# Attention and a feed-forward layer in one kernel: one head's softmax scaling in late turns goes from the vector engine to GpSimd, and head 1 is turned first

## The chip, the core and the metric

The kernel runs on one core of a Trainium2 chip. The core has five engines that each work through a queue of their own in order: TensorE (PE, matrix products; its weight loads are listed as PEld), the vector engine (DVE), ScalarE (ACT), GpSimd (POOL) and SyncE (SP, which here only issues DMAs). They meet through semaphores. The metric is the device time of one execution in microseconds; for the kernel before it is the median of three runs.

## The reference

Two stages, everything in fp32. Shapes: q, k and v are (8 batches, 8 heads, 576 positions, 64); w_in is (512, 2048), w_out is (2048, 512).

```python
scores = (q @ k.T) / 8                      # per batch and head, 576 x 576
mask   = (pos[:, None] // 64) >= (pos[None, :] // 64)
scores = where(mask, scores, -1e9)
attn   = exp(scores - max(scores))
attn   = attn / (sum(attn) + 1e-9)
x      = (attn @ v), heads side by side     # (4608, 512)
h      = x @ w_in
out    = (h * sigmoid(1.702 * h)) @ w_out   # (4608, 512)
```

The mask is causal by blocks of 64, so of a row of queries only the keys up to the end of its own block count.

## The kernel before

**Attention.** Heads go in pairs, and a pair is a turn: 32 turns, numbered n. The 576 queries of a head are cut in five chunks, 0 to 4; chunk i has 128 queries (chunk 0 has 64) and needs 64 x (2i + 1) keys, so chunk 4 needs all 576. For each chunk `score` puts the scores of both heads into PSUM, `weigh` applies mask and scale and takes the row's extreme on the vector engine (L351) and the exponential with its row sum on ScalarE (L358), and `normalise` adds 1e-9 to the sum, doubles it (which halves h, so that (1 + tanh(1.702 h/2)) h/2 is h x sigmoid) and takes the reciprocal on the vector engine (L368, L371) and multiplies each head's weights by it (L376 on GpSimd, L378 on the vector engine, L380 on ScalarE). The table `SCALE_ON` says which engine does that for each chunk, in three phases: turns 0 to 3, 4 to 7, and the 24 late turns from 8 on. Before the change GpSimd has all of it but chunk 4 of the late turns, where the vector engine scales both heads.

**Turning the weights.** The product with v needs the weights with the keys on the partitions. In the first eight turns TensorE transposes them. In the late turns `turn` does it: the vector engine transposes blocks of 32x32 into the tile `turned`, one instruction for each head (L385) and one for the diagonal blocks of both heads (L390), and after chunk 4 sixteen DMAs on SyncE's queue (L397) move the blocks to their places in the other half of `turned`. The next turn's `av` (60 matmuls) reads them there. Chunk 0 has no L385.

**Feed-forward.** It runs between the pieces of attention, in 12 tiles of 384 tokens and 16 chunks of 128 columns for each. For one such chunk TensorE makes 12 products into `hp`, ScalarE a tanh (L562), the vector engine `g = (g + 1) * hp` (L563); ScalarE splits off a high part `gh` (L571), GpSimd the low part `gl` (L82, through `subtract`), and TensorE adds 9 products of the chunk before into `acc`. There is one PSUM bank for `hp`, so the products of the next chunk wait until L563 has read the last.

**What sets the order.** A turn's items stand in strings, for late turns

```python
"3+0/2+1 - - - V - - 4 - - - L -"
```

that is: chunks 3 and 0 in one bank and 2 and 1 in the next, `av` of the turn before (V), chunk 4, and loading and turning the next pair's q and k (L, `prep`, whose vector work is L297). Feed-forward work fills the slots after a time plan (`quota`, `advance`). Matrix products are held to the order of the program (`mm`, `tr`). All other instructions are ordered on their engines by the framework's planner, which simulates the program and issues what is ready, by priority; priority is the place in the program, and L562, L563, L571 and `gl` are raised by `high_priority(offset=300)`.

Of the kernel before, what the change touches and what calls it, by code (L numbers as in the profile page):

```python
# [16 lines left out]

SCALE_ON = ("PPPPP", "PPPPP", "PPPPD")  # L20

# [17 lines left out]
def attention_moe_kernel(  # L41
# [10 lines left out]
    B, H, S, D = q.shape  # L52
    DM, DF = w_in.shape
    P = 128
# [23 lines left out]
    def phase(n):  # L78
        return 0 if n < HP else 1 if n < 2 * HP else 2
# [85 lines left out]
    def width(i):  # L165
        return BLK * (2 * i + 1)
# [138 lines left out]
    def score(n, banks):  # L305
# [25 lines left out]
        for chunks, part in zip(banks, todo):  # L331
            e = {}
            for i, hd, lo, hi, s in part:
                e[i] = weigh(n, i, hd, lo, hi, s, e.get(i))
            for i in chunks[::-1]:
                normalise(n, i, e[i])
                if not early(n):
                    turn(n, i, e[i])
# [25 lines left out]
    def normalise(n, i, e):  # L364
        _, sm = stats[n]
        m = BLK if i == 0 else P
        c = sm[0:m, i]
        nc.vector.tensor_scalar(  # L368
            out=c, in0=c, scalar1=1e-9, scalar2=2.0, op0=ALU.add, op1=ALU.mult
        )  # L370
        nc.vector.reciprocal(out=c, in_=c)  # L371
        on = SCALE_ON[phase(n)][i]
        for hd in range(2):
            x, sc = e[0:m, hd], c[:, hd : hd + 1]
            if on == "P":
                nc.gpsimd.tensor_tensor(out=x, in0=x, in1=sc.to_broadcast([m, width(i)]), op=ALU.mult)  # L376
            elif on == "D":
                nc.vector.tensor_scalar(out=x, in0=x, scalar1=sc, scalar2=None, op0=ALU.mult)  # L378
            else:
                nc.scalar.activation(out=x, in_=x, func=AF.Copy, scale=sc)  # L380

    def turn(n, i, e):

        for hd in range(2 if i else 0):
            nc.vector.transpose(  # L385
                out=tw[:, :, SLOT[i] : SLOT[i] + i, hd].rearrange("p b j c -> p j b c"),
                in_=e[:, hd, 0 : i * P],
            )
        r = slice(BLK, P) if i else slice(0, BLK)
        nc.vector.transpose(  # L390
            out=tw[r, 0:2, 9 + max(i, 1)].rearrange("p b h c -> p h b c"), in_=e[r, :, i * P : width(i)]
        )
        if i == NCH - 1:
            for kb in range(4):
                for qb in range(4):
                    ns = 10 if kb > 1 else NS if qb > 1 else 11
                    nc.sync.dma_start(  # L397
                        out=pw[kb * 32 : kb * 32 + 32, qb, 0:ns], in_=tw[qb * 32 : qb * 32 + 32, kb, 0:ns]
                    )
# [265 lines left out]
```

## Time and profile before

| | |
|---|---|
| time, median of 3 runs | 1122.79 us (1121.68 to 1124.22) |
| profiled execution: time, span | 1120.49 us, 1118.6 us |
| busy share of the span: PE, PEld | 96%, 81% |
| DVE, ACT, POOL | 52%, 45%, 36% |
| granted TensorE clock, mean over the span | 0.992 |
| DMA, mean over the span | 82 GB/s |

| stretch, us | what runs | PE busy | DVE busy | ACT busy | POOL busy |
|---|---|---|---|---|---|
| 0 to 195 | turns 0 to 7, weights made | 164.06 | 140.98 | 133.57 | 114.13 |
| 195 to 560 | late turns | 357.99 | 200.25 | 153.94 | 123.19 |
| 592.3 to 960 | late turns | 367.41 | 200.75 | 153.25 | 121.93 |
| 960 to 1118.6 | feed-forward alone | 154.59 | 24.09 | 45.49 | 36.59 |

Busy time is the time in which an engine has an instruction running. Instructions of one engine overlap a little at their ends, and matmuls are pipelined, so a TensorE that is always busy can still have lost some time: the distance between the starts of two neighbouring matmuls shows it better. A bracket at the end of a row of a timeline is idle time of the engine before it and what ended it; where several instructions of one kind follow each other without a gap the row merges them (x2, x3) and gives their time together. Numbers behind a line's name, as 128x576, are partitions by elements.

### The profile page before, as it was taken

The numbers are of one execution on the slowest core, as the hardware profiler recorded it, in microseconds if no ns is written. First come the engines' busy times: TensorE is split into PE (matmuls) and PEld (weight loads), VectorE is DVE, ScalarE is ACT, GpSimd is POOL, SyncE is SP. The second block draws the span as 40 slices with busy tenths as digits, with TensorE's granted clock in tenths as the row PEclk, the third lists the DMA queues.
The fourth block names the chain that finished last, engine by engine and source line by source line (L and its number), as shares of the span: only waits on it lengthen the run. The fifth ranks groups of instructions, "written<-read, shape, count | busy, mean of one in ns | idle before, by whom it ended". The sixth has DMA issues, their size and how long they took to land. (4 is left out here: it accounts for less than half of the span.)

```text
span 1118.6 us, 19977 instructions
## 1 busy us (share of the span) xinstructions
PE 1076.4 (96%) x6960; PEld 908.7 (81%) x6960; DVE 583.0 (52%) x1856; ACT 498.6 (45%) x1321; POOL 406.7 (36%) x509
## 2 busy tenths in 40 slices
PE   5969998999999999999999999999999999999998
PEld 3757776788888888888888888888888888899997
DVE  6776885545545555654555655645545654211210
ACT  5866776434534433534443543444434444322322
POOL 4665664333333332333333333333333233122222
PEclk9979999999999999999999999999999999999999
DMA  8734532332444432343443333344342332200000
GB/s 171 205 89 153 150 73 62 84 79 57 105 86 86 103 80 64 64 98 78 98 101 74 75 93 65 70 108 85 81 107 63 71 85 58 54 29 1 29 1 29
DMA packets 219365, 91.25 MB, mean 82 GB/s; under 512 B 197760, under 2 KB 197760, under 8 KB 219264
## 3 DMA queue, kind: packets, MB, share of 16 engines
q1 hardware_dynamic: 214528, 89.38, 34.0%
q10 hardware_dynamic: 4736, 0.59, 0.3%
q8 instruction: 55, 0.90, 0.3%
q14 instruction: 46, 0.38, 0.1%
HBM read 45.09 MB, written 9.44 MB: 49 GB/s over the span
## 5 line engine op out<-in xcount | busy, mean ns | idle before, releaser
L82 POOL TENSOR_TENSOR gl<-g,gh 128x384 fp32r<-128x384 f32 x192 | 194.7, 1014 | 551.5 <-ACT gh L571 449.1
L99 PE MATMUL hp<-xh,wih 128*128 128x384 f32 x768 | 264.7, 345 | 7.9 <-DVE g L563 6.9
L563 DVE SCALAR_TENSOR_TENSOR g<-g,hp 128x384 f32<-128x384 f32 x192 | 105.9, 552 | 319.1 <-ACT g L562 317.8
L99 PE MATMUL hp<-xh,wil 128*128 128x384 f32 x768 | 258.4, 336 | 0.1
L562 ACT ACTIVATE g<-hp 128x384 f32<-128x384 f32 x192 | 94.1, 490 | 359.8 <-PE hp L99 354.8
L99 PE MATMUL hp<-xl,wih 128*128 128x384 f32 x768 | 253.9, 338 | 0.4 <-DVE xl L82 0.4
L99 PE MATMUL acc<-woh,gh 128*128 128x512 f32 x576 | 233.9, 406 | 0.0
L99 PE MATMUL acc<-wol,gh 128*128 128x512 f32 x576 | 226.9, 394 | 0.0
L99 PEld LDWEIGHTS hp<-xh,wih 128*128 128x128 f32 x768 | 144.2, 188 | 34.1 <-DVE g L563 23.1
L99 PE MATMUL acc<-woh,gl 128*128 128x512 f32 x576 | 167.9, 393 | 0.3 <-POOL gl L82 0.3
L571 ACT CAST gh<-g 128x384 fp32r<-128x384 f32 x192 | 98.4, 513 | 156.5 <-DVE g L563 156.4
L99 PEld LDWEIGHTS hp<-xh,wil 128*128 128x128 f32 x768 | 144.3, 188 | 6.5 <-POOL wil L82 0.7
L358 ACT ACTIVATE e<-e,mx 64x64 f32<-64x64 f32 (+4 forms) x240 | 132.3, 552 | 37.6 <-DVE mx L351 37.6
L376 POOL TENSOR_TENSOR e<-e,sm 64x64 f32<-64x64 f32 (+1 forms) x192 | 113.6, 612 | 95.0 <-DVE sm L371 46.5
L99 PEld LDWEIGHTS hp<-xl,wih 128*128 128x128 f32 x768 | 143.6, 188 | 1.3 <-DVE xl L82 1.3
L99 PE MATMUL bank<-qk 64*128 64x320 f32 (+4 forms) x768 | 122.5, 428 | 14.5 <-DVE qk L297 11.1
L99 PEld LDWEIGHTS acc<-woh,gh 128*128 128x128 f32 x576 | 107.9, 187 | 34.2 <-issue 10.5
L99 PEld LDWEIGHTS acc<-woh,gl 128*128 128x128 f32 x576 | 107.8, 188 | 25.9 <-POOL gl L82 1.2
L99 PEld LDWEIGHTS acc<-wol,gh 128*128 128x128 f32 x576 | 108.3, 188 | 16.7 <-POOL wol L82 0.3
L351 DVE CUSTOM_DVE_ANT_0 e<-bank,mask 64x64 f32<-64x64 f32 (+4 forms) x240 | 89.7, 417 | 56.9 <-PE bank L99 52.8
L385 DVE STREAM_TRANSPOSE turned<-e 128x384 f32<-128x384 f32 (+1 forms) x192 | 92.3, 499 | 48.8 <-POOL e L376 48.3
L99 PEld LDWEIGHTS bank<-qk 64*128 64x128 f32 x768 | 69.6, 193 | 54.2 <-issue 25.4
(50 smaller groups left out, 956.0 us busy)
## 6 DMA issues: line engine op xcount, KB each, us to landing
turned<-turned SPq DMA_DIRECT2D x192, 80.0 KB, 2.1
turned<-turned SPq DMA_DIRECT2D x96, 112.0 KB, 2.2
raw<-in_q_dram SPq DMA_DIRECT2D x128, 72.0 KB, 2.4
out_dram<-osb SPq DMA_DIRECT2D x36, 256.0 KB, 2.2
raw<-in_k_dram SPq DMA_DIRECT2D x120, 72.0 KB, 2.6
turned<-turned SPq DMA_DIRECT2D x96, 88.0 KB, 2.1
words<-in_moe_w_in_dram SPq DMA_DIRECT2D x16, 512.0 KB, 6.3
vp<-in_v_dram SPq DMA_DIRECT2D x60, 128.0 KB, 2.4
```

The lines of the kernel that those rows point to most:

```text
L82: eng.tensor_tensor(out=out, in0=in0, in1=in1, op=ALU.subtract)
L99: return tc.keep_in_program_order(nc.tensor.matmul(**kw))
L351: nc.vector.tensor_tensor_reduce(out=e[0:m, hd, lo:hi], in0=s, in1=mk, op0=ALU.add, op1=ALU.min, scale=-0.125, scalar=3e38 if lo == 0 else ...
L358: nc.scalar.activation(out=e[0:m, hd], in_=e[0:m, hd], func=AF.Exp, scale=-1.0, bias=mx[0:m, i, hd : hd + 1], accum_out=sm[0:m, i, hd : hd ...
L376: nc.gpsimd.tensor_tensor(out=x, in0=x, in1=sc.to_broadcast([m, width(i)]), op=ALU.mult)
L385: nc.vector.transpose(out=tw[:, :, SLOT[i] : SLOT[i] + i, hd].rearrange("p b j c -> p j b c"), in_=e[:, hd, 0 : i * P],)
L562: nc.scalar.activation(out=g, in_=hp[:, 0:tt], func=AF.Tanh, scale=1.702)
L563: nc.vector.scalar_tensor_tensor(out=g, in0=g, scalar=1.0, in1=hp[:, 0:tt], op0=ALU.add, op1=ALU.mult)
L571: nc.scalar.copy(out=gh, in_=g)
```

## The change

In the late turns GpSimd multiplies head 0 of chunk 4 and the vector engine head 1; the letter M in the table stands for that. And `turn` takes head 1 before head 0, for all chunks from 1 to 4 of the late turns.

```diff
-SCALE_ON = ("PPPPP", "PPPPP", "PPPPD")
+SCALE_ON = ("PPPPP", "PPPPP", "PPPPM")
...
         on = SCALE_ON[phase(n)][i]
         for hd in range(2):
             x, sc = e[0:m, hd], c[:, hd : hd + 1]
-            if on == "P":
+            if on == "P" or on == "M" and hd == 0:
                 nc.gpsimd.tensor_tensor(out=x, in0=x, in1=sc.to_broadcast([m, width(i)]), op=ALU.mult)
-            elif on == "D":
+            elif on != "A":
                 nc.vector.tensor_scalar(out=x, in0=x, scalar1=sc, scalar2=None, op0=ALU.mult)
             else:
                 nc.scalar.activation(out=x, in_=x, func=AF.Copy, scale=sc)
 
     def turn(n, i, e):
 
-        for hd in range(2 if i else 0):
+        for hd in (1, 0) if i else ():
             nc.vector.transpose(
```

## Rows read from the trace of the kernel before

**Rows 1.** TensorE's waits, 195 to 960 us: engine, line, releaser, total us, times, longest.
```profile
PE hp L99 <- DVE g L563: 5.1, 6, 0.9
PEld hp L99 <- DVE g L563: 21.0, 40, 1.3
```

**Rows 2.** Vector engine, one turn's chunk 4: start, us, engine, line, tiles, count.
```profile
562.30 1.44 DVE L297 STREAM_TRANSPOSE qk<-raw 128x576 f32<-128x576 f32 x2
...
563.82 0.17 DVE L371 RECIPROCAL sm<-sm 128x2 f32<-128x2 f32 x1
564.02 0.95 DVE L378 TENSOR_SCALAR e<-e,sm 128x576 f32<-128x576 f32 x2
564.88 1.30 DVE L385 STREAM_TRANSPOSE turned<-e 128x512 f32<-128x512 f32 x2
566.21 0.31 DVE L390 STREAM_TRANSPOSE turned<-e 64x128 f32<-64x128 f32 x1
566.55 0.55 DVE L563 SCALAR_TENSOR_TENSOR g<-g,hp 128x384 f32<-128x384 f32 x1
```

**Rows 3.** TensorE in that turn: behind chunk 4, then an undisturbed stretch.
```profile
566.31 0.86 PE L99 MATMUL acc<-woh,gl 128*128 128x512 f32 x3
567.16 0.45 PE L99 MATMUL hp<-xh,wih 128*128 128x384 f32 x1
567.44 0.34 PE L99 MATMUL hp<-xh,wil 128*128 128x384 f32 x1
...
577.15 0.85 PE L99 MATMUL acc<-woh,gl 128*128 128x512 f32 x3
577.85 0.33 PE L99 MATMUL hp<-xh,wih 128*128 128x384 f32 x1
578.02 0.34 PE L99 MATMUL hp<-xh,wil 128*128 128x384 f32 x1
```

**Rows 4.** TensorE behind chunk 4 in an earlier turn.
```profile
277.07 0.86 PE L99 MATMUL acc<-woh,gl 128*128 128x512 f32 x3
278.78 0.45 PE L99 MATMUL hp<-xh,wih 128*128 128x384 f32 x1 [0.85 <-DVE g L563]
```

**Rows 5.** Chunk 2 of a turn: vector engine, and first GpSimd's line.
```profile
586.53 1.40 POOL L376 TENSOR_TENSOR e<-e,sm 128x320 f32<-128x320 f32 x2 [1.22 <-DVE sm L371]
586.22 0.17 DVE L371 RECIPROCAL sm<-sm 128x2 f32<-128x2 f32 x1
...
587.96 0.45 DVE L385 STREAM_TRANSPOSE turned<-e 128x256 f32<-128x256 f32 x1 [0.23 <-POOL e L376]
588.42 0.31 DVE L390 STREAM_TRANSPOSE turned<-e 64x128 f32<-64x128 f32 x1
588.76 0.55 DVE L563 SCALAR_TENSOR_TENSOR g<-g,hp 128x384 f32<-128x384 f32 x1
```

**Rows 6.** GpSimd's groups by shape, 0 to 195 us: busy us, mean ns.
```profile
L376 POOL TENSOR_TENSOR turned<-turned,sm 128x576 f32<-128x576 f32 x16 | 18.0, 1146 | 5.7 <-DVE sm L371 2.6 <-DVE mx L351 2.0 <-ACT xr L450 0.8
```

**Rows 7.** Meetings of the two engines, and the gl's duration min/median/max ns.
```profile
20.69 1.12 DVE L368 TENSOR_SCALAR sm<-sm 64x2 f32<-64x2 f32 x1
20.64 2.25 POOL L376 TENSOR_TENSOR turned<-turned,sm 128x576 f32<-128x576 f32 x2 [1.71 <-DVE sm L371]
212.48 0.95 DVE L378 TENSOR_SCALAR e<-e,sm 128x576 f32<-128x576 f32 x2
213.19 1.12 POOL L82 TENSOR_TENSOR gl<-g,gh 128x384 fp32r<-128x384 f32 x1 [5.54 <-ACT gh L571]
L82 POOL TENSOR_TENSOR gl<-g,gh x141: 991/1013/1117, 198.1 to 958.1; 128x384 fp32r<-128x384 f32 x141
```

**Rows 8.** The vector engine's waits, 195 to 960 us, as in rows 1.
```profile
DVE turned L385 <- POOL e L376: 48.3, 94, 1.1
```

**Rows 9.** SyncE's queue and TensorE behind chunk 4 of the turn in rows 2.
```profile
566.21 11.14 SPq L397 DMA_DIRECT2D turned<-turned  x16
580.04 2.99 PE L99 MATMUL bank<-turned,vp 128*64 128x128 f32 x60
```

## The prediction

> **What bounds the kernel now.** I read the busy shares first, then the windows by stage, then TensorE's waits in the late stretch, and last the instructions of single turns on each engine. TensorE is the bound: in the stretch of the late turns, from 195 to 960 us, there is next to nothing that it waits for except one thing. Before the first matrix product of a feed-forward chunk (hp) it waits for the vector engine's g step (L563), because there is one PSUM bank for hp and that step is the last reader of it; the matmul row has 6 such waits, the weight-load row 40 [rows 1]. So the edit can matter by one road only: what it does to the moment at which L563 gets its turn on the vector engine, which works through its queue in order.
>
> Two queues hold it up. The first is chunk 4's: reciprocal, two scalings, two wide transposes, the transpose of the diagonal, then L563 [rows 2]. The reader is to see that these stand one behind the other with no gap, and that L563 starts 0.03 us after the diagonal's transpose. What it costs TensorE is seen on its own rows [rows 3]. Undisturbed, the first hp product starts 0.70 us after the last three acc products begin (577.15 to 577.85), and the next 0.17 us later. Behind chunk 4 it is 0.85 us (566.31 to 567.16) and 0.28: 0.26 us lost. In other turns the same queue ends later against TensorE and 1.71 us pass (277.07 to 278.78) [rows 4], some 1.0 us lost at the start and 1.1 with the interval behind it. I went through the 24 late turns: the loss is there in 23, about 1.1 in 6 of them, 0.28 in 15, 0.15 in two; 6 x 1.13 + 15 x 0.28 + 2 x 0.15 = 11.3 us. The other queue is that of chunk 2, with L563 right behind its diagonal [rows 5]; in 17 turns it costs 0.15 to 0.4 us, 3.3 in all. 23 and 17 are the 40 waits. In all of these L563 is already late for TensorE, so a shift of L563 passes to the time one for one, later or (until the loss is gone) earlier.
>
> **The change, chunk 4.** Removed from the vector engine: one of two scalings a turn. The pair takes 0.95 us, and the next instruction starts 0.86 after the first of them, so one is worth 0.43 [rows 2]. Added: a GpSimd multiplication of 128x576, 1.146 us in the early turns, where GpSimd has all of chunk 4 [rows 6]; and a wait, of head 0's transpose for it. What stands behind that wait on the vector engine is head 0's transpose, the diagonal (which reads both heads) and L563. Step by step, with the turn at 564 us:
> - The reciprocal ends at 563.82 + 0.17 = 563.99. Head 1's scaling starts at 564.02 as now and, 0.95 - 0.43 = 0.52 long, ends at 564.54. Head 1's transpose starts 0.43 behind the scaling's start, at 564.45, and is over by 565.15.
> - GpSimd starts a scaling 0.14 us after the reciprocal's end (586.22 + 0.17 to 586.53) [rows 5], so head 0's at 564.13, behind the vector engine's scaling, and meets it for 0.41 us.
> - What such a meeting costs is shown once: a GpSimd gl of 1.013 median began at 213.19, 0.24 us before the end of a pair of these scalings (212.48 + 0.95 = 213.43), and took 1.117 [rows 7]. 0.24 of overlap cost 0.10, so the first 0.14 us of the GpSimd instruction need nothing that the vector engine holds. Bounds from these rows: between no slip and the whole overlap, 0.41. I take 0.41 - 0.14 = 0.27, from the one row of this very pair of engines and operations.
> - Head 0's scaling then ends at 564.13 + 1.146 + 0.27 = 565.55. The transpose follows 0.03 later (586.53 + 1.40 to 587.96 [rows 5]), at 565.58. The present pair of transposes takes 1.30, 0.65 each, and they overlap a little; for one alone I take 0.70, an estimate, to 566.28. The diagonal follows 0.01 later (587.96 + 0.45 to 588.42), at 566.29 to 566.30, against 566.21 now: 0.09 us later, and L563 with it.
>
> So the saved 0.43 us is spent by the wait: the vector engine idles some 0.4 us between the two heads' transposes. The sum: 23 turns x 0.09 = 2.1 us slower. With no slip it is 0.27 - 0.09 = 0.18 earlier, with the whole overlap 0.14 more, 0.23 later: -4 to +5 us are the bounds of this term.
>
> The Trainium skill, "SBUF — State Buffer", section "SBUF: two separate sides", has a lock in this place: a port pair of the vector engine and GpSimd, held for the whole instruction by whichever starts first, the other fully blocked. By that rule GpSimd's full 1.146 us would begin at 564.54, which gives 23 x 0.23 = 5.3 us. The row of the GpSimd gl shows less than full blocking, 0.10 for 0.24, so I stay with the row.
>
> What hides the rest: the sixteen DMAs behind the diagonal leave in 11.14 us from 566.21, and their reader, the 60 matmuls of the next turn, starts at 580.04 [rows 9]. 0.09 us later changes nothing there. GpSimd has 1.146 us x 24 = 28 us more to do; its next gl needs the result of L563, which comes later than the end of head 0's scaling.
>
> **The change, chunks 1 to 3.** The turning order is reversed for them too. If the queue took the program's order literally, head 1's transpose would wait for the second GpSimd scaling and head 0's would come after it. But the order on the engine is the planner's, which issues what is ready: in this trace the transposes of the next pair's queries and keys (L297), which the program has behind chunk 4, stand ahead of chunk 4's reciprocal [rows 2]. Nearly all of the transposes of chunks 1 and 2 wait for GpSimd, 94 waits [rows 8], so each is issued as it gets ready, and head 0 is ready first. I take no change here. From both sides: nothing below, since no work goes; above, one transpose's length per chunk, as in the third rival.
>
> **Rivals.**
> 1. GpSimd and the vector engine don't hold each other up here. For: only one row shows the slip. Against: it is this very scaling that caused it. L563 comes 0.18 earlier; 21 x 0.18 + 2 x 0.15 = 4.1 us faster, 1118.7. 12%.
> 2. The planner sees the wait of head 0's transpose and puts L563, which has a raised priority, into it. For: in two turns L563 already stands ahead of the diagonal. Against: in the other 22 it was put behind the whole queue, and the new queue is hardly longer. The most it can give is the 11.3 us of chunk 4's losses: 1111.5; ahead of the diagonal alone, 0.31 - 0.09 = 0.22 a turn, 5 us: 1118. 14%.
> 3. Slower: the new order binds in chunks 1 and 2. Head 1's transpose can't start before 587.96 as now, and head 0's 0.45 follows, so the diagonal and L563 move from 588.42 and 588.76 by 0.45 [rows 5]; chunk 1's, of a transpose shorter than that, is passed on, so up to 0.9. In 17 turns L563 is late there already: 7.7 to 15.3 us, with the 2.1 some 1133 to 1140. It decides as soon as head 0's transpose isn't issued in the gap before head 1's. 14%.
> 4. Slower: GpSimd starts first. A tiny scaling of the vector engine (L368) that began 0.05 us behind a GpSimd pair took 1.12 us: it waited out the whole first instruction (20.64 + 1.146 = 21.79, and it ends at 21.81) [rows 7]. If head 1's scaling met that, it would begin at 564.13 + 1.146 = 565.28 and head 1's transpose at 565.28 + 0.43 = 565.71, where the pair now begins at 564.88: 0.83 late, 23 x 0.83 = 19 us, 1142. Against: head 1's scaling follows the reciprocal on the same engine by 0.03 us, GpSimd by 0.14, and only an instruction put between them would turn that round. By the rule named above the first to start holds the other, too. 6%.
> 5. It does nothing: slip and saving cancel, or the planner's new order gives back what the wait costs. Within 1 us of now. 12%.
>
> **How the numbers follow.** The profiled execution took 1120.49 us (span 1118.6), 2.3 below the median of the runs, 1122.79. The sum of 2.1 on it gives 1122.6; on the median, 1124.9, which I predict (42%). Its own range, 0.04 to 0.15 us a turn, is 1123.7 to 1126.3. The range of 8 in 10 takes in rivals 1, 2 and 5 below and stops short of most of 3 and of 4: 1112 to 1131. About 0.2%, 2.25 us, is what a measurement can tell. Slower by more: rivals 3 and 4 (20%) and 18 of the forecast's 42, which lies just under that bound: 38%. Within: the other 24 and rival 5's 12: 36%. Faster: rivals 1 and 2, 26%.
>
> **What would show it.** In the changed profile: one L378 a turn, with head 1's transpose right behind it; an idle gap of some 0.4 us of the vector engine before head 0's, ended by GpSimd (L376); the 128x576 scaling at 1.40 to 1.45 us instead of 1.146 (no slip: 1.15, the lock's full price: 1.56); 23 losses of TensorE before L563 behind chunk 4, each about 0.09 longer; chunks 1 and 2 as in [rows 5]. I am wrong if L563 stands in another place of the queue, or if that scaling runs at 1.15.

## The result and the profile after

The change makes the kernel slower by about a quarter of a per cent: 1126.10 us (median of 9 runs, 1125.31 to 1128.57) against 1122.94 (9 runs) for the kernel before, a ratio of 1.0028, 95% interval 1.0017 to 1.0040, or 1.9 to 4.5 us. The profiled execution took 1125.38 us, its span is 1123.5.

First the two waits of TensorE that [rows 1] showed and the vector engine's wait of [rows 8] (kernel after, 197 to 965 us: releaser, total us, times, longest).

```profile
PE hp L99 <- DVE g L563: 6.2, 8, 1.0
...
PEld hp L99 <- DVE g L563: 23.6, 40, 1.5
...
DVE turned L385 <- POOL e L376: 55.3, 119, 1.1
```

TensorE's weight loads have 40 waits for L563 as before, and these have become longer in all, 21.0 to 23.6 us; the vector engine has 25 waits more for GpSimd, about one a turn. TensorE has no other new wait of that size. Next the two scalings of chunk 4 (kernel after: by line, duration min/median/max in ns, first and last start; then by group, busy us and mean ns).

```profile
L378 DVE TENSOR_SCALAR e<-e,sm x24: 520/521/1237, 214.9 to 955.7; 128x576 f32<-128x576 f32 x24
```
```profile
L376 POOL TENSOR_TENSOR e<-e,sm 128x576 f32<-128x576 f32 x24 | 33.3, 1386 | 37.6 <-DVE sm L371 37.6
```

One L378 a turn instead of two, and the GpSimd multiplication takes 1386 ns where the same shape undisturbed took 1146 [rows 6]. Now one turn, the one of [rows 2, 3]: the timelines of the vector engine, GpSimd and TensorE (kernel after).

```profile
567.35 0.17 DVE L371 RECIPROCAL sm<-sm 128x2 f32<-128x2 f32 x1
567.55 0.52 DVE L378 TENSOR_SCALAR e<-e,sm 128x576 f32<-128x576 f32 x1
568.10 0.71 DVE L385 STREAM_TRANSPOSE turned<-e 128x512 f32<-128x512 f32 x1
569.10 0.71 DVE L385 STREAM_TRANSPOSE turned<-e 128x512 f32<-128x512 f32 x1 [0.29 <-POOL e L376]
569.84 0.31 DVE L390 STREAM_TRANSPOSE turned<-e 64x128 f32<-64x128 f32 x1
570.18 0.55 DVE L563 SCALAR_TENSOR_TENSOR g<-g,hp 128x384 f32<-128x384 f32 x1
```
```profile
567.68 1.39 POOL L376 TENSOR_TENSOR e<-e,sm 128x576 f32<-128x576 f32 x1 [1.41 <-DVE sm L371]
```
```profile
569.84 0.86 PE L99 MATMUL acc<-woh,gl 128*128 128x512 f32 x3
570.79 0.44 PE L99 MATMUL hp<-xh,wih 128*128 128x384 f32 x1
571.07 0.34 PE L99 MATMUL hp<-xh,wil 128*128 128x384 f32 x1
```

Read them from left to right. The vector engine is done with head 1 at 568.81 and then stands idle 0.29 us until GpSimd hands over head 0. From the start of the reciprocal to the start of L563 it is 567.35 to 570.18, 2.83 us; before it was 563.82 to 566.55, 2.73 [rows 2]. TensorE passes the 0.10 on: from the last acc products to the first of hp 569.84 to 570.79, 0.95, where 0.85 stood [rows 3].

How that adds up is read from one line. L390, the diagonal's transpose, marks the late turns: its first execution opens them, its last one closes the last chunk 4. The kernel before and the kernel after (duration min/median/max in ns, first and last start in us):

```profile
L390 DVE STREAM_TRANSPOSE turned<-e x120: 295/308/311, 194.7 to 952.9; 64x128 f32<-64x128 f32 x120
```
```profile
L390 DVE STREAM_TRANSPOSE turned<-e x120: 297/308/311, 197.2 to 958.0; 64x128 f32<-64x128 f32 x120
```

The late stretch is 952.9 - 194.7 = 758.2 us before and 958.0 - 197.2 = 760.8 after: 2.6 us longer. What follows it is the same (1118.6 - 952.9 = 165.7, 1123.5 - 958.0 = 165.5). What precedes it differs by 2.5 us between these two executions, but it does so between executions of any of the kernels below (194.7 to 199.7, once 199.2 in a kernel with the time of before); the mean granted clock there is 0.96 of full speed in the one and 0.94 in the other. So spans are not compared here, but this stretch is.

Two more places. Chunk 2 of the kernel after, against [rows 5] (vector engine):

```profile
589.82 0.17 DVE L371 RECIPROCAL sm<-sm 128x2 f32<-128x2 f32 x1
590.88 0.45 DVE L385 STREAM_TRANSPOSE turned<-e 128x256 f32<-128x256 f32 x1 [0.90 <-POOL e L376]
591.56 0.45 DVE L385 STREAM_TRANSPOSE turned<-e 128x256 f32<-128x256 f32 x1 [0.23 <-POOL e L376]
...
592.36 0.55 DVE L563 SCALAR_TENSOR_TENSOR g<-g,hp 128x384 f32<-128x384 f32 x1
```

2.54 us from reciprocal to L563, as before (586.22 to 588.76): the reversed order does nothing here. And a turn in which L563 stood ahead of the diagonal, the kernel before and then the kernel after:

```profile
725.11 0.17 DVE L371 RECIPROCAL sm<-sm 128x2 f32<-128x2 f32 x1
...
727.40 0.52 DVE L563 SCALAR_TENSOR_TENSOR g<-g,hp 128x384 f32<-128x384 f32 x1
```
```profile
729.19 0.17 DVE L371 RECIPROCAL sm<-sm 128x2 f32<-128x2 f32 x1
...
731.70 0.31 DVE L390 STREAM_TRANSPOSE turned<-e 64x128 f32<-64x128 f32 x1
732.04 0.55 DVE L563 SCALAR_TENSOR_TENSOR g<-g,hp 128x384 f32<-128x384 f32 x1
```

There the planner has put L563 behind the diagonal: 2.29 became 2.85. That happened in two turns.

### The profile page after: what moved, and what is told of

Its sections match the earlier page's. It is cut to its first block, busy times and chain, and to the rows that moved or that the text cites. A ratio compares the mean times of both kernels' runs of the same rounds, so it can differ in the third digit from the quotient of the medians.

```text
span 1123.5 us, 19999 instructions
## 1 busy us (share of the span) xinstructions
PE 1079.4 (96%) x6960; PEld 910.5 (81%) x6960; DVE 578.9 (52%) x1832; ACT 498.9 (44%) x1321; POOL 440.0 (39%) x533
## 5 line engine op out<-in xcount | busy, mean ns | idle before, releaser
L563 DVE SCALAR_TENSOR_TENSOR g<-g,hp 128x384 f32<-128x384 f32 x192 | 106.0, 552 | 318.9 <-ACT g L562 317.6
L376 POOL TENSOR_TENSOR e<-e,sm 64x64 f32<-64x64 f32 (+4 forms) x216 | 146.8, 698 | 133.7 <-DVE sm L371 83.2
L385 DVE STREAM_TRANSPOSE turned<-e 128x384 f32<-128x384 f32 (+1 forms) x192 | 95.3, 505 | 56.1 <-POOL e L376 55.3
```

The costliest lines, as they stand in the source:

```text
L385: nc.vector.transpose(out=tw[:, :, SLOT[i] : SLOT[i] + i, hd].rearrange("p b j c -> p j b c"), in_=e[:, hd, 0 : i * P],)
L563: nc.vector.scalar_tensor_tensor(out=g, in0=g, scalar=1.0, in1=hp[:, 0:tt], op0=ALU.add, op1=ALU.mult)
```

## The experiments

My theory: the time follows the start of L563 behind chunk 4, and this is now set by a chain over GpSimd (reciprocal, slowed scaling of head 0, head 0's transpose, diagonal), which is longer than the queue that it replaces by 0.10 us. Against it stood: the turning order costs the time (rival 3 of the prediction), the order of the start decides (rival 4), the meeting of the two engines costs nothing (rival 1), or an earlier L563 isn't worth anything to TensorE at all. "In order" in the edits below holds head 0's wide transpose of chunk 4 behind head 1's, so that the planner can't turn them round when a piece gets shorter:

```diff
-            nc.vector.transpose(
+            d = nc.vector.transpose(
...
-            )
+            ); i == NCH - 1 and hd == 0 and tc.keep_in_program_order(d)
```

No kernel has this hold alone. With the short scaling and with 448 and 320 columns the vector engine's instructions from chunk 4's reciprocal to L563 stand in the order of the change in all 24 turns, so there the hold changed no order.

All together, with three numbers for each: how L563 stands against the kernel before in one undisturbed turn (from the reciprocal's start, 2.73 us [rows 2]), the late stretch against 758.2 us, and the median against that of the kernel before on the same chip.

| kernel | L563 in one turn, us | late stretch, us | medians, us |
|---|---|---|---|
| after | +0.10 | +2.6 | +3.2 |
| old turn order | +0.11 | +2.6 | +3.7 |
| turn order alone | +0.01 | -0.2 | +0.3 |
| scaling nearly left out | -0.27 | -6.2 | -5.4 |
| one head on ScalarE | -0.30 | -6.4 | -5.9 |
| short scaling beside | -0.12 | -2.6 | -3.4 |
| GpSimd 448 columns | -0.10 | -2.3 | -1.7 |
| GpSimd 320 columns | -0.29 | -6.2 | -6.2 |
| ScalarE in chunks 4 and 2 | -0.30, chunk 2 -0.35 | -11.2 | -11.5 |
| GpSimd first | +0.17 | +3.4 | +3.4 |
| GpSimd first by more | +0.58 | +12.8 | +11.7 |

(For the last the turn is counted from the end of L297, 2.81 before and 3.39 here, since its reciprocals stand elsewhere.) Twenty-three turns times the first column gives the second to within 1 us wherever only chunk 4's work was changed.

**The old turn order.** The change with head 0 turned first again in the program.

```diff
-        for hd in (1, 0) if i else ():
+        for hd in range(2 if i else 0):
```

> The split of chunk 4's scaling as in the change (head 0 on GpSimd, head 1 on the vector engine), but `turn` takes head 0 before head 1 as before. Theory (the wait of head 0's transpose for GpSimd is the whole price, the planner turns head 1 first by itself because it is ready first): as the change, some 1126 us, head 0's scaling again 1.39 to 1.41 us, each L563 behind chunk 4 again 0.10 us later than before the change. Rival (the reversed order of chunks 1 to 3 costs the time): as before the change, 1123 us. Second rival (the reversal is what makes the split bearable): head 0 turned first, the queue 0.5 us longer, some 12 us slower than before, 1135.

1126.57 us (5 runs) against 1122.91, ratio 1.0033 (1.0021 to 1.0045).

```profile
L390 DVE STREAM_TRANSPOSE turned<-e x120: 297/308/311, 196.9 to 957.7; 64x128 f32<-64x128 f32 x120
```

760.8 us, that of the change. Moving the scaling is the whole effect; the planner turns head 1 first in chunk 4 anyway, because it is ready first.

**The turn order alone.** The kernel before with (1, 0).

```diff
-        for hd in range(2 if i else 0):
+        for hd in (1, 0) if i else ():
```

> Only the turning order is reversed; the vector engine scales both heads of chunk 4 as before. Theory: no difference to before beyond 1 us, since chunks 1 and 2 are still turned as their heads get ready and chunk 3's both heads are ready. Rival (the order binds in chunks 1 to 3): 3 us slower, all of what the change costs, or more: up to 13 us if chunk 2's L563 moves by 0.45 to 0.77 us.

1123.16 us (12 runs), ratio 1.0001 (0.9990 to 1.0011).

```profile
L390 DVE STREAM_TRANSPOSE turned<-e x120: 297/308/311, 199.2 to 957.2; 64x128 f32<-64x128 f32 x120
```

758.0 us: nothing. Rival 3 falls, in both kernels.

**A scaling nearly left out.** The kernel before, head 0 of chunk 4 scaled in 64 of its 576 columns.

```diff
-                nc.vector.tensor_scalar(out=x, in0=x, scalar1=sc, scalar2=None, op0=ALU.mult)
+                y = width(i) if hd else BLK; nc.vector.tensor_scalar(out=x[:, 0:y], in0=x[:, 0:y], scalar1=sc, scalar2=None, op0=ALU.mult)
```

> The kernel before, but of head 0's 576 columns of chunk 4 only 64 are scaled, on the vector engine; the other 512 are left unscaled. So the vector engine saves most of one scaling and waits for nobody. Theory (L563's turn on the vector engine is all that matters, the saved scaling is worth 0.43 us less some 0.12 for the short one): L563 0.3 us earlier behind chunk 4, 6 x 0.3 + 15 x 0.28 + 2 x 0.15 = 6 us faster than before, 1117. Rival (the late stretch is bound by TensorE alone and chunk 4's queue is hidden; the change is slower for another reason): no difference to before.

1117.47 us (6 runs), ratio 0.9951 (0.9939 to 0.9963).

```profile
L390 DVE STREAM_TRANSPOSE turned<-e x120: 295/308/311, 196.5 to 948.5; 64x128 f32<-64x128 f32 x120
```

752.0 us. So the time taken off the vector engine's queue does pass to TensorE, 0.27 us a turn: the saving is there to be had, and in the change the wait eats it.

**One head on ScalarE.** The change, but head 0 goes to ScalarE and not to GpSimd.

```diff
-            if on == "P" or on == "M" and hd == 0:
+            if on == "P":
...
-            elif on != "A":
+            elif on == "D" or on == "M" and hd:
```

> As the change, but ScalarE instead of GpSimd scales head 0 of chunk 4, and the vector engine head 1. ScalarE should take some 0.75 us and be done before the vector engine has turned head 1, so head 0's transpose waits for nobody, and ScalarE does not meet the vector engine. Theory: the full 0.43 us of the scaling is saved, L563 0.4 earlier behind chunk 4: 6 x 0.43 + 15 x 0.28 + 2 x 0.15 = 7 us faster than before, 1116; where ScalarE does the scaling ahead of a tanh, part of that is lost. Rival (any split that adds a wait across engines costs what the change costs): 1126. Rival (ScalarE's tanh and gh come later by the 0.75 us): slower than before, by 23 x 0.4 = 9 us, 1132.

1116.99 us (6 runs), ratio 0.9946 (0.9933 to 0.9960): faster than both. Its turn, vector engine and ScalarE:

```profile
563.53 0.17 DVE L371 RECIPROCAL sm<-sm 128x2 f32<-128x2 f32 x1
563.74 0.52 DVE L378 TENSOR_SCALAR e<-e,sm 128x576 f32<-128x576 f32 x1
564.29 1.30 DVE L385 STREAM_TRANSPOSE turned<-e 128x512 f32<-128x512 f32 x2
565.63 0.31 DVE L390 STREAM_TRANSPOSE turned<-e 64x128 f32<-64x128 f32 x1
565.96 0.55 DVE L563 SCALAR_TENSOR_TENSOR g<-g,hp 128x384 f32<-128x384 f32 x1
```
```profile
563.79 0.78 ACT L380 ACTIVATE e<-e,sm 128x576 f32<-128x576 f32 x1 [0.50 <-DVE sm L371]
```

ScalarE starts 0.09 us after the reciprocal, not 0.16, needs 0.78 us, not 1.39, and doesn't slow the scaling beside it (0.52). It ends at 564.57, before head 1's transpose is over, so the transposes follow each other without a gap. Here is also the size of the saving: head 1's transpose starts 0.55 us behind the scaling, where the pair's started 0.86 behind [rows 2]: 0.31, not the 0.43 of the prediction. The weight loads' waits for L563 (190 to 975 us) show how far it carries:

```profile
PEld hp L99 <- DVE g L563: 12.2, 25, 1.1
```

25 are left of 40. In 15 turns the loss behind chunk 4 is gone: in the one above, the first hp product starts 0.70 us after the last acc products (566.02 to 566.72) and the next 0.17 later, as undisturbed [rows 3]. In those turns a still earlier L563 would bring nothing.

**A short scaling beside.** The change, but the vector engine scales only columns 448 to 575 of head 1; transposes in order.

```diff
-                nc.vector.tensor_scalar(out=x, in0=x, scalar1=sc, scalar2=None, op0=ALU.mult)
+                nc.vector.tensor_scalar(out=x[:, 448:576], in0=x[:, 448:576], scalar1=sc, scalar2=None, op0=ALU.mult)
```

> As the change, but the vector engine scales only the last 128 of head 1's 576 columns of chunk 4 (the other 448 are left unscaled), and head 0's transpose is held behind head 1's. GpSimd's scaling of head 0 is whole. Theory (GpSimd's scaling is slowed by meeting the vector engine's, by the overlap less 0.14 us): with a scaling of some 0.25 us there is hardly an overlap beyond 0.14, so head 0's scaling is back at 1.15 to 1.17 us from 1.39 to 1.41, and L563 comes 0.25 earlier than in the change: 23 x 0.25 = 5.7 us, 1120. Rival (that scaling is slow for another reason, as its place in the tile or the broadcast factor): 1.39 to 1.41 again and 1126.

1119.71 us (6 runs) against 1123.08, ratio 0.9967 (0.9952 to 0.9983). GpSimd's group and the marker:

```profile
L376 POOL TENSOR_TENSOR e<-e,sm 128x576 f32<-128x576 f32 x24 | 28.0, 1165 | 37.6 <-DVE sm L371 36.2 <-PE hp L99 1.4
```
```profile
L390 DVE STREAM_TRANSPOSE turned<-e x120: 296/308/311, 194.7 to 950.3; 64x128 f32<-64x128 f32 x120
```

The vector engine has less to do here, but head 0's transpose still waits for GpSimd. What has gone is the meeting: 1165 ns instead of 1386, and L563 comes 0.22 earlier than in the change. The slip of 0.24 us is thus what makes the change slower and not faster.

**GpSimd 448 and 320 columns.** The change, but GpSimd scales only so many columns of head 0; in order.

```diff
-                nc.gpsimd.tensor_tensor(out=x, in0=x, in1=sc.to_broadcast([m, width(i)]), op=ALU.mult)
+                y = width(i) if on == "P" else 448; nc.gpsimd.tensor_tensor(out=x[:, 0:y], in0=x[:, 0:y], in1=sc.to_broadcast([m, y]), op=ALU.mult)
```

> As the change, but GpSimd scales only 448 of head 0's 576 columns of chunk 4 (128 are left unscaled), and head 0's transpose is held behind head 1's, which keeps the order of the change. Theory (the end of GpSimd's scaling sets when head 0's transpose starts): 448 columns take 0.933 us instead of 1.146 without the meeting, so L563 comes 0.21 earlier than in the change, in 23 turns 4.9 us: 1121, a little below before. Rival (the wait for another engine costs a fixed time, whatever the length): 1126.

> The same with 320 columns (256 are left unscaled). Theory: 0.72 + 0.27 us end before head 1's transpose does, so head 0's follows it without a gap, as with one head on ScalarE: the losses behind chunk 4 fall to those of that kernel, 1117. Rival (a fixed price of the wait): 1126.

1121.42 us (12 runs), ratio 0.9985 (0.9974 to 0.9996), and 1116.90 (5 runs), 0.9949 (0.9935 to 0.9962). The wide transposes and GpSimd's scaling with 448 and then with 320 columns:

```profile
568.55 1.50 DVE L385 STREAM_TRANSPOSE turned<-e 128x512 f32<-128x512 f32 x2
...
568.13 1.18 POOL L376 TENSOR_TENSOR e<-e,sm 128x448 f32<-128x448 f32 x1 [1.41 <-DVE sm L371]
```
```profile
564.31 1.31 DVE L385 STREAM_TRANSPOSE turned<-e 128x512 f32<-128x512 f32 x2
...
563.89 0.96 POOL L376 TENSOR_TENSOR e<-e,sm 128x320 f32<-128x320 f32 x1 [1.41 <-DVE sm L371]
```

At 448 columns the pair of transposes still has a gap (1.50 us), at 320 it is as tight as in the kernel before (1.31 to 1.30 [rows 2]). There the time is that of the ScalarE kernel and of the scaling nearly left out, 1117: GpSimd's length no longer counts, and the saved scaling is worth all that it can be. The change would have brought these 6 us if GpSimd needed no more than about 1 us for its head (an estimate: with 320 columns it needs 0.96), and it needs 1.39.

**ScalarE in chunks 4 and 2.** The kernel with one head on ScalarE, and chunk 2's head 1 there too, head 0 on GpSimd.

```diff
-SCALE_ON = ("PPPPP", "PPPPP", "PPPPM")
+SCALE_ON = ("PPPPP", "PPPPP", "PPNPM")
...
-            if on == "P":
+            if on == "P" or on == "N" and hd == 0:
```

> A version of use: as the kernel with head 0 of chunk 4 on ScalarE and head 1 on the vector engine, and in chunk 2 of the late turns ScalarE takes head 1 and GpSimd keeps head 0, so that the two heads are scaled side by side. Theory (L563 behind chunk 2 is late too, by 0.15 us or more in 17 turns): chunk 2's diagonal comes some 0.25 us earlier and those losses go, 3 to 4 us on top of the 5.9: 1113 to 1114. Rival (ScalarE, which also makes tanh and gh, becomes late by its extra 0.5 us): as that kernel or slower, 1117 to 1120.

1111.59 us (4 runs) against 1123.08, ratio 0.9903 (0.9887 to 0.9919): the best of all. TensorE's waits, then one chunk 2 on GpSimd and ScalarE:

```profile
PEld hp L99 <- DVE g L563: 4.5, 9, 0.7
```
```profile
585.05 0.72 POOL L376 TENSOR_TENSOR e<-e,sm 128x320 f32<-128x320 f32 x1 [1.22 <-DVE sm L371]
...
585.00 0.56 ACT L380 ACTIVATE e<-e,sm 128x320 f32<-128x320 f32 x1 [1.62 <-DVE sm L371]
```

The heads are scaled side by side where GpSimd's pair took 1.40 us [rows 5], and of the 40 waits 9 are left. The two queues of the prediction are thus the two that cost, by experiment. Chunk 2 brought more than was expected, 4.8 us by the late stretch (11.2 less 6.4) where 3 to 4 were: in the six turns with the large loss the one behind chunk 4 shrinks too, in the first of them from 1.38 us between the starts of the last acc products and the first hp product to 1.05. There chunk 4's reciprocal follows chunk 2's by 6.00 us (240.88 to 246.88), where it was 6.33 with one head on ScalarE (238.83 to 245.16).

**GpSimd first, and by more.** Both are the change with chunk 4's reciprocal as two instructions, head 0's first, so that GpSimd could start while the vector engine is busy with the other; in order. The second also splits the addition ahead of it and puts head 1's behind head 0's reciprocal. The edit of the first, without the hold:

```diff
-        nc.vector.reciprocal(out=c, in_=c)
+        for y in (c[:, 0:1], c[:, 1:2]) if SCALE_ON[phase(n)][i] == "M" else (c,): nc.vector.reciprocal(out=y, in_=y)
```

> As the change, but chunk 4's reciprocal of the late turns is two instructions, head 0's first, and head 0's transpose is held behind head 1's. GpSimd, which starts 0.14 us after head 0's reciprocal, then begins before the vector engine's scaling of head 1, which has head 1's reciprocal of some 0.17 us ahead of it. Theory (whichever of the two scalings starts first makes the other wait; so far the vector engine's did, by 0.11 us): GpSimd's is back at 1.146 us, the vector engine's takes 1.2 to 1.4 us instead of 0.52, head 1's transpose starts some 1.0 us later, and L563 some 0.64 later than in the change: 23 x 0.64 = 15 us, 1141. Rival (the two only slow each other a little, whoever comes first): GpSimd's at 1.4 again, the vector engine's at 0.52 and the time that of the change plus 23 x 0.15 for the second reciprocal, 1129.

1127.22 us (6 runs) against 1123.80, ratio 1.0039 (1.0025 to 1.0053). A miss: the kernel didn't do what it was built for. Its vector engine and GpSimd:

```profile
567.68 0.23 DVE L371 RECIPROCAL sm<-sm 128x1 f32<-128x1 f32 x2
567.94 0.52 DVE L378 TENSOR_SCALAR e<-e,sm 128x576 f32<-128x576 f32 x1
```
```profile
568.01 1.45 POOL L376 TENSOR_TENSOR e<-e,sm 128x576 f32<-128x576 f32 x1 [1.41 <-DVE sm L371]
```

The two reciprocals overlap, 0.23 us for both, and the scaling follows at once: GpSimd starts 0.07 us behind it, not before it. It only shows the slip at a larger overlap: 0.45 us, and 1.45 instead of 1.146.

> As the kernel with two reciprocals, where the two reciprocals ran into each other and GpSimd still came second, but the addition ahead of the reciprocal (L369) is two instructions too, and head 1's is held behind head 0's reciprocal. So head 1's scaling starts some 0.4 us behind head 0's reciprocal and GpSimd's, at 0.14, before it. Theory (the one that starts first makes the other wait): GpSimd's scaling takes 1.146 to 1.2 us; the vector engine's, 0.52 so far, ends some 0.3 us behind GpSimd's end and so takes 1.1 to 1.3; head 1's transpose starts only then, the two transposes stand behind it without a gap, and L563 comes 0.5 to 0.64 later than in the change: 23 x 0.5 to 0.64 = 11 to 15 us, 1137 to 1141. Rival (the two only slow each other by 0.3 us, whoever comes first): the vector engine's scaling 0.8 us or less and the time that of the change within some 4 us, 1122 to 1130.

1136.09 us (4 runs) against 1124.41, ratio 1.0106 (1.0089 to 1.0122): a little under the 1137 to 1141 of the theory, and far from its rival. Vector engine, GpSimd, and the marker:

```profile
573.51 0.12 DVE L371 RECIPROCAL sm<-sm 128x1 f32<-128x1 f32 x1
573.55 0.13 DVE L369 TENSOR_SCALAR sm<-sm 128x1 f32<-128x1 f32 x1
573.72 0.16 DVE L371 RECIPROCAL sm<-sm 128x1 f32<-128x1 f32 x1
573.92 1.35 DVE L378 TENSOR_SCALAR e<-e,sm 128x576 f32<-128x576 f32 x1
575.30 1.30 DVE L385 STREAM_TRANSPOSE turned<-e 128x512 f32<-128x512 f32 x2
```
```profile
573.80 1.15 POOL L376 TENSOR_TENSOR e<-e,sm 128x576 f32<-128x576 f32 x1 [1.28 <-DVE sm L369]
```
```profile
L390 DVE STREAM_TRANSPOSE turned<-e x120: 296/308/310, 199.0 to 970.0; 64x128 f32<-64x128 f32 x120
```

Now GpSimd is 0.12 us ahead, runs its 1.15 undisturbed, and the vector engine's scaling takes 1.35 us instead of 0.52: it ends 0.32 us after GpSimd does. The late stretch is 771.0 us, 12.8 longer than before. Who starts first pays nothing, and the change is on the cheaper side of that by 0.13 us (567.55 to 567.68). Rival 4 is a real mechanism, only not the one of this change; the prediction priced it at 0.83 us a turn, and this kernel shows 0.58.

The Trainium skill, "SBUF — State Buffer", section "SBUF: two separate sides", has the first to start hold the shared port pair for its whole instruction and the other blocked in full, where the vector engine's instruction is in a 2-port mode or has two SBUF inputs. The runs agree in who pays and not in how much. With GpSimd first the scaling of 0.52 us takes 1.35: it loses 0.83 of an overlap of 1.03 us (573.92 to 574.95). With the vector engine first GpSimd loses 0.24 of 0.39 us in the change, and full blocking would make that 0.39.

## Why the prediction held, step by step

| step | predicted | measured |
|---|---|---|
| vector engine's and GpSimd's start after the reciprocal's end, us | 0.03, 0.14 | 0.03, 0.16 |
| overlap of the two scalings | 0.41 | 0.39 |
| slip of GpSimd's | 0.27 | 0.24 |
| head 0's transpose after the reciprocal's end | 1.59 | 1.58 |
| idle of the vector engine before that | 0.4 | 0.29 |
| from that start to the diagonal | 0.71 | 0.74 |
| L563 later, one turn | 0.09 | 0.10 |
| all turns | 2.1 | 2.6 in the late stretch; 3.2 (1.9 to 4.5) by medians |

The measured 1126.1 lies in the forecast's own range, and the chain is the one that was forecast. The slip was the term that decided the sign, and it came from a single row, a gl that had met the same scaling [rows 7]. One row could have misled; the slips of the kernels below the change in the table bear it out. Without a meeting the change gains, as the short scaling shows; with full blocking, 0.39 for 0.24, it would have lost some 0.15 us a turn more (an estimate). The step from L563 to the end, one for one in 23 turns until the loss is gone, is borne out by every kernel in the table, in both directions.

Two terms were off. The start of head 1's transpose, 0.43 us behind the scaling, is 0.55: I took the worth of a saved scaling from how closely two independent scalings follow each other, while a transpose that needs the scaling's result waits for its end. Here that cost nothing, because head 0's transpose waits for GpSimd until after head 1's is done; in the kernels where the saving decides it is 0.27 to 0.30 a turn, and a forecast with 0.43 would have been some 40% too high. And two turns in which L563 stood ahead of the diagonal lost that place and cost 0.56 us, not 0.09: some 0.9 us more for both. By the prediction's own sign, L563 in another place of the queue, it was wrong in these two. With 23 x 0.10 that would be 3.2 us and the stretch shows 2.6, so other turns gave some back: in one, near 438 us, the tanh comes 0.46 us later after the reciprocal than before (435.02 to 435.52, and 437.77 to 438.73), TensorE with it, and the loss is 0.35 smaller. So the stretch's 2.6 holds misses that go opposite ways, and that it lies as near to 2.1 is in part luck. Why the planner moved L563 in the two turns was not followed up.

Two small slips of the prediction changed nothing. The upper end of its own range is 1122.79 + 23 x 0.15 = 1126.2, not 1126.3. And L563 stood behind the whole queue in 21 turns, not in "the other 22": the first late turn has it elsewhere.

In that first late turn the meeting went the other way (kernel before, vector engine; kernel after, vector engine and GpSimd):

```profile
212.03 0.53 DVE L563 SCALAR_TENSOR_TENSOR g<-g,hp 128x384 f32<-128x384 f32 x1
212.48 0.95 DVE L378 TENSOR_SCALAR e<-e,sm 128x576 f32<-128x576 f32 x2
```

```profile
214.48 0.53 DVE L563 SCALAR_TENSOR_TENSOR g<-g,hp 128x384 f32<-128x384 f32 x1
214.93 1.24 DVE L378 TENSOR_SCALAR e<-e,sm 128x576 f32<-128x576 f32 x1
...
214.71 1.15 POOL L376 TENSOR_TENSOR e<-e,sm 128x576 f32<-128x576 f32 x1 [4.59 <-DVE sm L371]
```

L563 had come between the reciprocal and the scaling, the very thing that rival 4 needed, and it stood there before the change too, so the trace already had the place where rival 4 would come true. It cost nothing there, since no L563 stood right behind.

Of the rivals, 1 falls by the 1386 ns and 5 by the interval. 2 falls by the timelines: the planner didn't use the new gap of 0.29 us in any turn, and where it moved L563 it moved it back. 4 came true in the first late turn alone. 3 falls by the kernel with the turn order alone.

## What to carry to other kernels

Before a piece of work goes to an idle engine, compare when its result arrives at the join with when the busy engine would have had it; a busy share saved counts only up to that moment. If the other piece runs at the same time, look in the trace for a place where these two engines met on these operations, and ask which of them starts first. Of two idle engines take the one that ends first and doesn't slow the neighbour: here ScalarE, 0.78 us against 1.39, turned a loss of 3 us into a gain of 6.

## What the runs showed of the hardware

- A GpSimd multiplication that starts inside a vector-engine scaling loses the overlap less 0.13 to 0.15 us: 0.24 of 0.39 us (change), 0.25 of 0.39 (448 columns, 0.933 alone), 0.24 of 0.38 (320 columns, 0.720 alone), 0.30 of 0.45 (GpSimd first), 0.02 of 0.15 (short scaling). With 576, 448 and 320 columns the price is the same, so it doesn't depend on GpSimd's own length.
- The other way round the vector engine's scaling of 576 columns ends 0.32 us after GpSimd's multiplication, whether it began 0.12 us behind it (573.92) or 0.22 (214.93; 0.31), and whether GpSimd's had 576 columns or 320 (first late turn of that kernel: 214.84 + 0.72 = 215.56 and 215.07 + 0.81 = 215.88). It loses the overlap less some 0.2 us: 0.83 of 1.03 us, and 0.29 of 0.49.
- Two independent reciprocals of 128x1 take 0.23 us together, against 0.17 for one of 128x2: splitting it brought GpSimd's start no nearer, 0.33 us after the first reciprocal's start in both (567.35 to 567.68, change; 567.68 to 568.01, GpSimd first).
- On the vector engine a transpose that needs the scaling just ahead of it starts 0.03 us after that ends; two scalings that need nothing of each other overlap by 0.09 (0.95 for two of 0.52).
